# A planned kernel (mLSTM and a gated feed-forward layer): another picture of transposing transfers, the output's store on another engine, and the order found anew

## The chip, the cores and the metric

The kernel runs on one core of one Trainium2 chip. The metric is the device time of one execution in microseconds (us). A core has engines that run side by side, each through its own list of instructions in program order: PE (TensorE, the matmuls), DVE (VectorE), ACT (ScalarE), POOL (GpSimd) and SP (SyncE, which here only issues DMA transfers). They wait for each other by semaphores.

## The reference

Two parts follow each other. First an mLSTM for B = 4 batches, H = 8 heads, S = 768 steps and head size D = 40:

```python
for t in range(S):
    m_new = np.maximum(f_gate[:, :, t] + m, i_gate[:, :, t])
    f_stab = np.exp(f_gate[:, :, t] + m - m_new)
    i_stab = np.exp(i_gate[:, :, t] - m_new)
    C = f_stab * C + i_stab * np.einsum('bhd,bhe->bhde', vt, kt)
    n = f_stab * n + i_stab * kt
    h_tilde = np.einsum('bhde,bhe->bhd', C, qt)
    denom = np.maximum(np.abs(np.einsum('bhd,bhd->bh', n, qt)), 1.0)
    y[:, :, t] = sigmoid(o_gate) * h_tilde / denom
```

Then, for each of the 3072 tokens x (320 wide, all heads side by side):

```python
h = x @ w_in                                 # 320 -> 1024
e = np.exp(h - h_max)
solu = h * e / (e.sum() + 1e-9)
ln = (solu - mu) / np.sqrt(var + 1e-6) * g_ln
out = ln @ w_out                             # 1024 -> 320
```

## The kernel before

**Units.** The sequence is cut into 6 chunks of 128 steps. A unit u is one batch's chunk: 128 tokens, all 8 heads; there are 24, the batch running fastest, so unit u needs the state that unit u − 4 left. In each unit (line numbers of the kernel before):

- tk (L917) loads the tokens' values, keys and queries; el and er (L920, L930) load gate sums from DRAM. DVE reduces tk to the queries' size (am, L962), ACT and DVE cast the queries into a high and a low half (qs, L982 and L990), and a transposing DMA brings them into qT (L1006).
- d: PE makes the exponents of the gates in two groups of four heads (L1021) in psum buffers named sy, ACT takes the exponential (L1033), POOL masks it (L1047). PE makes the scores (L1092), DVE multiplies them with the masks (L1104), and PE makes the inter-chunk part from the state (y, L1129) and the intra-chunk part (L1155). DVE divides (x, L1193), and POOL multiplies with the output gate's sigmoid sg (L1205); the sigmoid is taken once for four units (L1064).
- The state: PE's update (L1220) goes into the psum buffer sx. DVE copies it in two halves into cs (L1248), and POOL and two DMA copies finish it. There is one buffer sx, and the transposes of x (L1284) use it too. ACT and DVE cast the transposed x into a high half xh (L1289, L1290) and a low half xl (L1295, L1303).
- The feed-forward layer: 16 matmuls into ph (L1338), DVE's row maximum nm (L1395), ACT's exponential e (L1402), DVE's sums and product (s, sb from L1411; e, L1456), ACT's squares sq (L1467), DVE's short z and ab (L1477 to L1480). POOL raises to the power −1/2 (pw, L1488). ACT casts the result to half precision (us, L1526), POOL makes the low part (L1502), and a transposing DMA brings both into big (L1505). 24 matmuls go into the psum buffer so_ (L1542; one buffer), ACT scales that into ot (L1564), and a DMA stores it (L1569).

The weights are loaded and split ahead of it, in blocks: w_in, and w_out (L747 loads, L632 casts on ACT, L788 is DVE's centring, eight operations).

**The order.** Nothing is emitted where it is written. Each piece is recorded with `P.op` on an engine, with a duration in ns, what it writes and reads, and a priority. `Plan.run` then simulates the engines: it takes the engine whose next piece can start first, and of the pieces on it that could start within 25 ns of each other the one of lowest priority. Each engine's program is the order so found, and the chip keeps to it. The priority is `rank`: the table RANK has three numbers for each kind of work, one for all units, one weighted to the first four and one weighted to the last four. When a buffer comes round again, the plan makes its next user wait for all users of the last.

DMA has a picture of its own in the plan: an issue on its engine for some ns, and for all transfers together one "dma" time, to which each transfer adds its `after`. A transposing transfer is marked swift. `load` records an ordinary one.

While the weights are prepared the plan also puts matmuls of no use on idle PE (L1583): 65 of them, before and after the change alike.

Of the kernel before, what the change touches and what calls it, by code (L numbers as in the profile page):

```python
# [49 lines left out]
RANK = {  # L50
    "dve hv": (-8.77, 9.26, 4.82),
    "act dl": (0.78, 2.31, -4.35),
    "sp cs": (0.07, -14.3, 2.82),
# [11 lines left out]
    "sp qT": (-13.44, -12.38, -6.71),
    "act d": (-5.4, -18.84, 4.87),
    "pool kt": (45.57, 11.55, -3.27),
    "pe ps": (6.61, 6.35, 2.41),
    "dve p": (-10.23, 3.52, -0.65),
    "pe sy": (-15.11, 18.49, 0.7),  # L70
    "dve y": (10.14, -9.76, 58.33),
    "dve rd": (11.26, -29.28, -6.47),
    "dve yi": (-27.2, 3.12, 7.54),
    "dve x": (-13.73, 20.42, 8.34),
    "pool x": (14.62, 16.05, -18.49),
    "pe sx": (17.0, -10.7, -3.08),
    "pool ct": (9.82, 3.17, -12.23),
    "dve cs": (3.16, 13.11, -5.46),
    "pool cs": (4.66, 7.11, -21.22),
    "pool c": (20.35, 9.11, -0.97),  # L80
    "act xh": (-12.03, -10.17, 10.98),
    "dve xl": (-2.53, 7.81, -4.99),
    "pe ph": (8.0, 18.89, 1.01),
    "dve us": (-8.44, -1.71, -1.62),
    "dve s": (21.3, 0.3, -5.21),
    "dve nm": (1.05, 9.93, -11.02),
    "act e": (12.47, -4.96, 3.73),
    "dve e": (9.73, -0.84, 5.75),
    "act sq": (13.33, -14.19, 1.37),
    "dve z": (-7.83, -3.7, -12.59),  # L90
    "dve ab": (6.33, 8.39, -12.11),
    "pool pw": (23.96, -7.55, 0.11),
    "dve so": (3.54, 5.69, 11.85),
    "act us": (-22.64, -5.39, -9.02),
    "pool us": (9.91, 12.1, -2.77),
    "sp big": (-4.83, -9.5, -2.73),
# [1 line left out]
    "act ot": (13.32, -27.18, 14.42),
    "sp ot": (-7.0, -11.66, 1.0),
    "sp w_in": (10.76,),  # L100
    "sp w_out": (-3.76,),
    "w_in": (-10.15,),
    "w_out": (-19.4,),
    "w_mul": (7.44,),
}
# [9 lines left out]
class Plan:  # L115
# [51 lines left out]
    def run(self):  # L167
# [174 lines left out]
def mlstm_moe_kernel(ctx: ExitStack, tc: tile.TileContext, tok, og, fg, ig, w_in, w_out, gln, out):  # L342
    nc = tc.nc
# [555 lines left out]
    def unit(u):  # L899
# [103 lines left out]
        op(
            SPQ,
            2500,
            lambda P: nc.sync.dma_start_transpose(  # L1006
# [204 lines left out]
        if c < NC - 1:  # L1211
# [313 lines left out]
        else:  # L1525
            op(ACT, 945, lambda P: nc.scalar.copy(out=P[us[0]][:, 0], in_=P[e]), [(*us[0], 0)], [e])  # L1526
# [42 lines left out]
        P.op(SPQ, 440, lambda P: nc.sync.dma_start(out=out[r : r + L, :], in_=P[ot]), [], [ot], rank(SPQ, "ot"), 440)  # L1569

# [58 lines left out]
```

## Time and profile before

| | |
|---|---|
| runs | 324.87, 323.91, 327.02 us; median 324.87 |
| profiled execution | 324.0 us, its span 322.3 us (1.7 us lie around it) |
| mean granted TensorE clock | 0.995 |
| busy: PE, DVE, ACT, POOL | 289.1, 270.3, 215.2, 172.0 us |
| DMA | 54.75 MB in 116498 packets, mean 170 GB/s |

In the rows of the trace SPq is SP's DMA queue, PEld PE's weight loads. A row begins with the start and length in us; a bracket at its end has the idle time of the engine ahead of it and what ended that. A line of the list of groups has the number of instructions, their busy time and the mean ns of one, and the idle time ahead.

### The profile page before, as it was taken

The page shows a single profiled execution, that of the slowest core. Times are in us where ns is not written, and L with a number is a line of the kernel's source. Part 1 is how long each engine was busy: PE and PEld are TensorE (multiplying, and loading weights), DVE is VectorE, ACT ScalarE, POOL GpSimd, SP SyncE. Part 2 cuts the span into 40 slices and gives each one's busy share as a digit, 9 for nine tenths or more (in the row PEclk, how much of TensorE's full clock was granted, in tenths as well). Part 3 has the DMA queues.
Part 4 walks back from the last instruction along what each step waited for, and adds up shares of the span by engine and source line. Part 5 has one row for each costly group of instructions (what it writes and reads, how often), then busy time and mean ns, then how long its engine had stood idle before and what let it go on. Part 6 is the DMA issues. An engine that isn't in the chain of part 4 may idle for free. (4 is left out here: it accounts for less than half of the span.)

```text
span 322.3 us, 6940 instructions
## 1 busy us (share of the span) xinstructions
PE 289.1 (90%) x2453; PEld 230.1 (71%) x2453; DVE 270.3 (84%) x702; ACT 215.2 (67%) x372; POOL 172.0 (53%) x193
## 2 busy tenths in 40 slices
PE   0499997989799997999989999999999999999965
PEld 0398774767588876688868778876888788777743
DVE  5995899999899888699987899986999979877540
ACT  4556966598975586775587757678655976665341
POOL 6002424457586844696673986474968534554300
PEclk9999999999999999999999999999999999999979
DMA  6789873564999987778979679796999776661631
GB/s 169 284 198 246 277 161 112 133 127 127 165 210 172 253 174 166 169 159 243 177 194 158 159 167 243 157 201 160 155 229 224 185 166 143 104 134 30 140 73 57
DMA packets 116498, 54.75 MB, mean 170 GB/s; under 512 B 103024, under 2 KB 110736, under 8 KB 116464
## 3 DMA queue, kind: packets, MB, share of 16 engines
q1 hardware_dynamic: 116464, 54.32, 75.9%
q8 instruction: 19, 0.31, 0.4%
q14 instruction: 15, 0.12, 0.2%
HBM read 21.66 MB, written 4.33 MB: 81 GB/s over the span
## 5 line engine op out<-in xcount | busy, mean ns | idle before, releaser
L1502 POOL TENSOR_TENSOR us<-e,us 128x1024 f16<-128x1024 f32 x23 | 49.3, 2142 | 57.8 <-ACT us L1526 52.1
L1542 PEld LDWEIGHTS <-big 128*128 128x128 f16 x576 | 60.0, 111 | 23.4 <-issue 4.3
L1155 PEld LDWEIGHTS sy<-tk,d 128*128 128x128 f32 x384 | 51.7, 192 | 3.8 <-DVE d L1104 1.4
L1155 PE MATMUL sy<-tk,d 128*128 128x41 f32 x384 | 52.0, 259 | 0.7 <-DVE d L1104 0.7
L982 ACT ACTIVATE qs<-tk,rr 128x640 f16<-128x640 f32 x48 | 37.6, 820 | 16.6 <-DVE rr L975 16.0
L1047 POOL TENSOR_SCALAR_AFFINE_SELECT d<-d 128x1024 f32<-128x1024 f32 x24 | 27.7, 1155 | 32.9 <-ACT dl L1043 32.0
L1205 POOL TENSOR_TENSOR x<-x,sg 128x320 f32<-128x320 f32 x24 | 23.0, 956 | 25.0 <-ACT d L1033 15.7
L1104 DVE SCALAR_TENSOR_TENSOR d<-sy,am,d 128x512 f32<-128x512 f32 x48 | 33.8, 745 | 1.8 <-POOL d L1047 1.3
L1033 ACT ACTIVATE d<-sy 128x512 f32<-128x512 f32 x48 | 28.2, 589 | 9.3 <-PE sy L1021 9.0
L1338 PE MATMUL ph<-wih,xh 128*128 128x512 f32 x96 | 32.1, 412 | 2.3 <-ACT xh L1290 2.1
L1526 ACT CAST us<-e 128x1024 f16<-128x1024 f32 x23 | 24.0, 1044 | 14.2 <-issue 4.3
L990 DVE SCALAR_TENSOR_TENSOR qs<-tk,rr,qs 128x320 f16<-128x320 f32 x48 | 29.2, 626 | 3.2 <-ACT qs L982 3.1
L1338 PE MATMUL ph<-wil,xh 128*128 128x512 f32 x96 | 30.3, 393 | 0.0
L1402 ACT ACTIVATE e<-ph,nm 128x1024 f32<-128x1024 f32 x23 | 25.5, 1109 | 6.8 <-DVE nm L1395 6.7
L1456 DVE SCALAR_TENSOR_TENSOR e<-ph,s,e 128x1024 f32<-128x1024 f32 x23 | 29.4, 1276 | 0.1
L1395 DVE TENSOR_REDUCE nm<-ph 128x1 f32<-128x1024 f32 x23 | 27.9, 1215 | 1.2 <-PE ph L1338 1.2
L1467 ACT ACTIVATE sq<-e,nmean 128x1024 bf16<-128x1024 f32 x24 | 27.5, 1144 | 0.6 <-DVE nmean L1446 0.6
L1338 PE MATMUL ph<-wih,xl 128*128 128x512 f32 x96 | 26.7, 398 | 0.0
L962 DVE TENSOR_REDUCE am<-tk 128x1 f32<-128x640 f32 x24 | 19.4, 810 | 3.3 <-DMA tk<-in_tok_dram 3.3
L1338 PEld LDWEIGHTS ph<-wih,xh 128*128 128x128 f32 x96 | 17.0, 189 | 6.6 <-ACT xh L1290 3.4
L1021 PE MATMUL sy<-er,el 128*128 128x512 f32 x48 | 20.8, 437 | 0.8 <-DMA er<-gd 0.5
L1338 PEld LDWEIGHTS ph<-wil,xh 128*128 128x128 f32 x96 | 18.0, 188 | 4.3
(199 smaller groups left out, 698.1 us busy)
## 6 DMA issues: line engine op xcount, KB each, us to landing
tk<-in_tok_dram SPq DMA_DIRECT2D x24, 484.0 KB
sg<-in_og_dram SPq DMA_DIRECT2D x12, 320.0 KB
out_dram<-ot SPq DMA_DIRECT2D x24, 160.0 KB
big<-in_w_out_dram SPq DMA_DIRECT2D x4, 640.0 KB
cs<-cs SPq DMA_DIRECT2D x20, 102.5 KB
big<-in_w_in_dram SPq DMA_DIRECT2D x4, 512.0 KB
cs<-c SPq DMA_DIRECT2D x20, 51.2 KB
big<-in_w_in_dram SPq DMA_DIRECT2D x2, 256.0 KB
```

Of the source, the lines that this page charges most:

```text
L982: nc.scalar.activation(out=dst, in_=q_src(P, a).unsqueeze(2).to_broadcast([L, H, 2, D]), func=AF.Copy, scale=P[rr],)
L990: V.scalar_tensor_tensor(out=q_parts(P, a, 2 - a, 1), in0=q_src(P, a), scalar=P[rr], in1=q_parts(P, a, 0, 1), op0=ALU.mult, op1=ALU.subtract,)
L1033: lambda P, j=j, pd=pd: nc.scalar.activation(out=P[d_t][:, 4 * j : 4 * j + 4, :], in_=P[pd].rearrange("p (h l) -> p h l", l=L), func=AF.Exp,),
L1047: lambda P: nc.gpsimd.affine_select(out=P[d_t], in_=P[d_t], pattern=[[0, H], [1, L]], base=0, channel_multiplier=-1, compare_op=ALU.is_ge, ...
L1104: lambda P, j=j, ps=ps: V.scalar_tensor_tensor(out=P[p_t][:, 4 * j : 4 * j + 4, :], in0=P[ps].rearrange("p (h l) -> p h l", l=L), scalar=P ...
L1155: nc.tensor.matmul(yv(P)[:, h, :], lhsT=P[p_t][:, h, :], rhs=v1(P)[:, h, :], start=True, stop=True)
L1338: nc.tensor.matmul(P[ph][:, j * HF : (j + 1) * HF], lhsT=a, rhs=w[:, j * HF : (j + 1) * HF], start=n == 0, stop=n == 7,)
L1395: lambda P: V.tensor_reduce(out=P[nm], in_=P[ph], axis=AX.X, op=ALU.max, negate=True),
L1456: lambda P: V.scalar_tensor_tensor(out=P[e], in0=P[ph], scalar=P[sc], in1=P[e], op0=ALU.mult, op1=ALU.mult, accum_out=P[nmean]),
L1467: lambda P: nc.scalar.activation(out=P[sq], in_=P[e], func=AF.Square, bias=P[nmean], scale=-float(DFF), accum_out=P[su]),
L1502: eng.tensor_tensor(out=P[us[1]][:, 1, sl], in0=P[e][:, sl], in1=P[us[0]][:, 0, sl], op=ALU.subtract)
L1542: nc.tensor.matmul(P[po][:, 0:DM], lhsT=uTv(P, a)[:, k, :], rhs=P[w][:, k, :], start=g == 0 and i == 0, stop=g == 3 and i == len(some) - 1,)
```

## The change

The change has three parts, all in what the plan is told. The matmuls, their sizes and all other operations are the same in number and kind; the store alone is on another engine.

1. The plan's costs of DMA: a transposing transfer occupies the issuing SP for 1950 ns instead of 2500 (2600 for big), adds 2600 ns to the "dma" time instead of 2300, and holds SP until at most 1000 ns of "dma" time are left (DMA_LAST). Some issues and copies get other costs.
2. The output's store is issued by ACT (`nc.scalar.dma_start`) instead of SP.
3. RANK has new numbers in every row, and the row "sp ot" gives way to "act st". Two of its 54 rows are shown.

```diff
 RANK = {
...
-    "dve am": (11.35, -12.35, 10.1),
+    "dve am": (9.58, 14.08, 13.41),
...
-    "pe so_": (141.04, -13.8, -12.79),
+    "pe so_": (13.4, -5.9, -1.95),
...
+    DMA_LAST = 1000
...
                 if self.swift[n]:
                     free["dma"] = max(max(s + self.DMA_IN, t) + after, end + self.DMA_IN + self.DMA_SWIFT)
+                    free[eng] = max(end, free["dma"] - self.DMA_LAST)
...
     def load(ns, fn, out, inp=(), prio=0.0, behind=(), issue=450, eng=SPQ):
-        P.op(eng, issue if eng == SPQ else 100, fn, out, inp, prio, ns, 1.0, behind)
+        P.op(eng, issue if eng == SPQ else 240, fn, out, inp, prio, ns, 1.0, behind)
...
-        load(1500, lambda P: nc.sync.dma_start(out=P[tk], ...), [tk], issue=650, ...)
+        load(1700, lambda P: nc.sync.dma_start(out=P[tk], ...), [tk], issue=500, ...)
...
         op(
             SPQ,
-            2500,
+            1950,
             lambda P: nc.sync.dma_start_transpose(
...
-            after=2300,
+            after=2600,
             swift=True,
         )
...
-            op(PE, 500, upd, [pu], [kt, tk])
+            op(PE, 350, upd, [pu], [kt, tk])
...
-            load(300, lambda P: nc.sync.dma_start(out=P[cn][D : 2 * D], in_=P[cn][0:D]), ...
+            load(430, lambda P: nc.sync.dma_start(out=P[cn][D : 2 * D], in_=P[cn][0:D]), ...
...
-            op(SPQ, 2600, lambda P: tr_u(P, 0, 0, 2 * DFF), [uT[0]], ..., after=2300, swift=True)
+            op(SPQ, 1950, lambda P: tr_u(P, 0, 0, 2 * DFF), [uT[0]], ..., after=2600, swift=True)
...
-        P.op(SPQ, 440, lambda P: nc.sync.dma_start(out=out[r : r + L, :], in_=P[ot]), [], [ot], rank(SPQ, "ot"), 440)
+        load(480, lambda P: nc.scalar.dma_start(out=out[r : r + L, :], in_=P[ot]), [], [ot], eng=ACT, prio=rank(ACT, "st"))
```

How it moves the instructions is shown at four places. Line numbers of the changed kernel are 3 higher from L300 on.

**DVE, unit 7.** cs is unit 7's new state, copied in two halves out of sx, am the reduction of unit 10's tokens, nm, sb, s and ab belong to earlier units' feed-forward layers, d to a later unit's masked scores. Before:

```order
L1395 TENSOR_REDUCE nm<-ph 128x1
L1248 TENSOR_TENSOR cs_1553<-ct,sx 40x4x41
L962 TENSOR_REDUCE am<-tk 128x1
L1248 TENSOR_TENSOR cs_1553<-ct,sx 40x4x41
L1104 SCALAR_TENSOR_TENSOR d<-sy,am,d 128x512 x2
```

After:

```order
L1398 TENSOR_REDUCE nm<-ph 128x1
L1251 TENSOR_TENSOR cs_1556<-ct,sx 40x4x41
L1414 TENSOR_SCALAR sb<-nm 128x1
L1483 TENSOR_SCALAR ab<-z,su 128x1
L1251 TENSOR_TENSOR cs_1556<-ct,sx 40x4x41
L1420 TENSOR_SCALAR sb<-nm,sb 128x1
L1107 SCALAR_TENSOR_TENSOR d<-sy,am,d 128x512 x2
L1426 RECIPROCAL s<-sb 128x1
L965 TENSOR_REDUCE am<-tk 128x1
```

The reduction has left the place between the halves and stands behind the masked scores; two one-column operations stand between the halves.

**PE, unit 8.** so_ is the output of an earlier unit, ph unit 8's feed-forward layer, sy<-cs unit 9's inter-chunk part, sy<-tk,d its intra-chunk part, sy<-er,el the first exponents of unit 10. Before, from the last output matmul on:

```order
L1542 MATMUL so__1726<-woh,big 128x320
L1338 MATMUL ph<-wih,xh 128x512 x2
L1338 MATMUL ph<-wil,xh 128x512 x2
L1338 MATMUL ph<-wih,xh 128x512 x2
L1338 MATMUL ph<-wil,xh 128x512 x2
L1129 LDWEIGHTS qT
L1129 MATMUL sy<-cs_1194,qT 128x41
```

After, where the sixteen matmuls of the inter-chunk part and twelve of the intra-chunk part stand ahead of these rows, between the output matmuls:

```order
L1545 MATMUL so__1717<-woh,big 128x320
L1158 MATMUL sy<-tk,d 128x41 x4
L1024 MATMUL sy<-er_97,el_110 128x512
L1341 MATMUL ph<-wih,xh 128x512 x2
L1341 MATMUL ph<-wil,xh 128x512 x2
L1341 MATMUL ph<-wih,xh 128x512 x2
L1341 MATMUL ph<-wil,xh 128x512 x2
```

ph has moved behind unit 9's two parts and unit 10's first exponents.

**ACT, around unit 7's store.** ot is the scaled output, qs a later unit's queries, d its exponentials, us and sq belong to the feed-forward layer. Before:

```order
L1526 CAST us<-e 128x1024
L1467 ACTIVATE sq,su<-e,nmean 128x1024
L1564 ACTIVATE ot<-so__1726,so 128x320
L982 ACTIVATE qs_77<-tk,rr 128x8x80
L1033 ACTIVATE d<-sy 128x512
L982 ACTIVATE qs_77<-tk,rr 128x8x2x40
L1033 ACTIVATE d<-sy 128x512
```

After:

```order
L1567 ACTIVATE ot<-so__1717,so 128x320
L985 ACTIVATE qs_77<-tk,rr 128x8x80
L1036 ACTIVATE d<-sy 128x512
L1529 CAST us<-e 128x1024
L1572 DMA out_dram<-ot 128x320
L985 ACTIVATE qs_77<-tk,rr 128x8x2x40
L1470 ACTIVATE sq,su<-e,nmean 128x1024
L1036 ACTIVATE d<-sy 128x512
```

The store stands three instructions behind the one that makes its data, and ahead of the second half of qs, the squares and the second exponential.

**DVE, the warm-up.** wg holds the weights being centred, e is the feed-forward product: unit 1's x stands ahead of the centring before, and unit 0's e 21 rows behind it. Before:

```order
L1193 TENSOR_TENSOR x<-sy,rd 128x320
L962 TENSOR_REDUCE am<-tk 128x1
L788 SCALAR_TENSOR_TENSOR wg<-wg,g,so__415 128x320 x8
L1104 SCALAR_TENSOR_TENSOR d<-sy,am,d 128x512 x2
```

After, where x is unit 2's and e unit 0's:

```order
L1255 COPY cs_630<-sx 40x4x41
L1196 TENSOR_TENSOR x<-sy,rd 128x320
L1459 SCALAR_TENSOR_TENSOR e,nmean<-ph,s,e 128x1024
L791 SCALAR_TENSOR_TENSOR wg<-wg,g,so__433 128x320 x8
L807 TENSOR_REDUCE wmx<-wm 128x1
```

Unit 2's x and unit 0's e now come ahead of the centring.

More of the change, by code (lines that the diff above doesn't have):

```diff
@@ L65 @@
[L65 to L96, printed above, removed]
-    "pe so_": (141.04, -13.8, -12.79),
[L98 to L104, printed above, removed]
+    "dve hv": (23.33, 2.61, -8.41),
+    "act dl": (-13.89, 1.42, 15.86),
+    "sp cs": (15.71, -11.0, 1.49),
+    "sp el": (11.68, 7.73, 7.44),
@@ new lines @@
+    "sp er": (-14.42, 10.81, -1.73),
+    "pe d": (-7.78, -13.43, 0.84),
+    "pool d": (-3.94, 7.63, -1.66),
+    "sp tk": (-1.91, 3.44, 1.44),
+    "sp sg": (10.11, -8.82, 1.07),
+    "act sg": (12.05, 13.77, 6.95),
+    "dve am": (9.58, 14.08, 13.41),
+    "dve rr": (-44.3, 6.12, -5.12),
+    "act qs": (4.5, 10.92, 1.85),
+    "dve qs": (5.02, -8.56, 4.35),
+    "sp qT": (-10.03, -9.06, -9.39),
+    "act d": (-5.33, 1.71, -3.54),
+    "pool kt": (2.84, 7.78, -9.82),
+    "pe ps": (1.88, 9.06, 7.84),
@@ new lines @@
+    "dve p": (-14.56, -5.61, 13.82),
+    "pe sy": (-16.95, 18.59, -2.67),
+    "dve y": (20.48, -15.63, 7.53),
+    "dve rd": (-9.54, -6.86, 8.01),
+    "dve yi": (4.0, -10.27, 27.79),
+    "dve x": (-12.07, -11.05, -10.34),
+    "pool x": (-11.54, -1.11, -11.0),
+    "pe sx": (1.75, -7.41, -9.99),
+    "pool ct": (-1.29, 6.93, -5.48),
+    "dve cs": (-10.37, 16.2, -0.21),
+    "pool cs": (13.28, -7.65, -8.37),
+    "pool c": (9.07, 5.8, 12.81),
+    "act xh": (6.31, -4.21, -10.37),
+    "dve xl": (2.01, 1.31, 12.34),
@@ new lines @@
+    "pe ph": (-1.6, 13.15, 11.88),
+    "dve us": (-4.93, 0.64, 0.84),
+    "dve s": (9.63, 19.53, -15.99),
+    "dve nm": (-4.22, 13.66, -14.95),
+    "act e": (4.37, 4.67, -4.78),
+    "dve e": (23.45, -18.54, 13.22),
+    "act sq": (12.59, 7.72, -4.31),
+    "dve z": (12.84, -14.02, -0.14),
+    "dve ab": (14.29, 4.79, -5.46),
+    "pool pw": (14.77, -10.21, 9.54),
+    "dve so": (-7.85, 12.93, 8.07),
+    "act us": (-10.4, 22.99, 9.12),
+    "pool us": (3.79, 3.14, 6.37),
+    "sp big": (-5.11, -1.19, 6.47),
@@ L105 @@
+    "pe so_": (13.4, -5.9, -1.95),
+    "act ot": (8.14, 7.42, -15.22),
+    "act st": (6.77, 11.98, 2.63),
+    "sp w_in": (8.91,),
+    "sp w_out": (7.71,),
+    "w_in": (-1.64,),
+    "w_out": (-9.29,),
+    "w_mul": (-5.17,),
 }
@@ L914, in op @@
             P.op(eng, ns, fn, o, i, rank(eng, o[0][0]), after, busy, behind, mix, port, swift)
-        load(1500, lambda P: nc.sync.dma_start(out=P[tk], in_=tok[b, c * L : (c + 1) * L, :]), [tk], issue=650, prio=rank(SPQ, "tk"), behind=[("d", u - 2)] if u > 1 else [])
+        load(1700, lambda P: nc.sync.dma_start(out=P[tk], in_=tok[b, c * L : (c + 1) * L, :]), [tk], issue=500, prio=rank(SPQ, "tk"), behind=[("d", u - 2)] if u > 1 else [])
         load(
@@ L1273, in unit @@
             )
-            load(300, lambda P: nc.sync.dma_start(out=P[cn][D : 2 * D], in_=P[cn][0:D]), [(*cn, 2)], [(*cn, 0), (*cn, 1)], issue=830, prio=rank(SPQ, "cs"))
+            load(430, lambda P: nc.sync.dma_start(out=P[cn][D : 2 * D], in_=P[cn][0:D]), [(*cn, 2)], [(*cn, 0), (*cn, 1)], issue=830, prio=rank(SPQ, "cs"))
             load(200, lambda P: nc.sync.dma_start(out=P[cn][2 * D :, 0], in_=P[c3]), [(*cn, 3)], [c3], issue=830, prio=rank(SPQ, "cs"))
@@ L1527, in unit @@
             op(POOL, 2105, lambda P: lo_u(P, nc.gpsimd, slice(0, DFF)), [(*us[1], 1)], [e, (*us[0], 0)])
-            op(SPQ, 2600, lambda P: tr_u(P, 0, 0, 2 * DFF), [uT[0]], [(*us[0], 0), (*us[0], 1)], after=2300, swift=True)
+            op(SPQ, 1950, lambda P: tr_u(P, 0, 0, 2 * DFF), [uT[0]], [(*us[0], 0), (*us[0], 1)], after=2600, swift=True)
         po, ot = (("so_", u), ("ot", u))
```

13 lines of the change are left out of this document (removed).

## The prediction

> **What bounds the kernel now.** I read the page first (busy shares and the digit rows), then busy time by stages of 10 us, then TensorE's own rows with the idle time in front of them, and last the waits of the DMA queue.
>
> ```profile
> PE 289.1 (90%) x2453; PEld 230.1 (71%) x2453; DVE 270.3 (84%) x702; ACT 215.2 (67%) x372; POOL 172.0 (53%) x193
> DVE  5995899999899888699987899986999979877540
> 50.00:60.00 10.00, 7.80 (x59) 5.88 (x60) 9.89 (x33) 4.76 (x12) 4.03 (x5) 1.00 0.11 33
> 150.00:160.00 10.00, 10.00 (x98) 8.15 (x97) 9.35 (x27) 6.05 (x13) 7.66 (x8) 1.00 1.05 205
> ```
>
> The stage rows give, after the stretch and its length, the busy time of PE, weight loads, DVE, ACT and POOL with their counts, then the granted clock, the DMA share and GB/s. In the steady stage (150 to 160) PE is busy the whole 10.00 us, and DVE 9.35: PE sets the pace, and only two things can move the end there, PE's instructions and the idle time in front of them. The change leaves PE's instructions as they are. In the warm-up (50 to 60) it is the other way round: PE 7.80, DVE 9.89. There the order of DVE's work sets the pace. PE's idle time is 33.2 us (the span of 322.3 less 289.1); most of it is the start and the end. What lies between are these rows (start, length, engine, line, operation, and in brackets the idle time in front and what ended it):
>
> ```profile
> 121.47 0.82 DVE L962 TENSOR_REDUCE am<-tk 128x1 f32<-128x640 f32 x1 [1.11 <-DMA tk<-in_tok_dram]
> 122.32 0.33 DVE L1248 TENSOR_TENSOR cs<-ct,sx 40x164 f32<-40x164 f32 x1
> 122.79 0.30 PE L1284 MATMUL sx<-ident,x 128*128 128x128 f32 x1 [1.76 <-DVE cs L1248]
> 168.11 0.30 PE L1284 MATMUL sx<-ident,x 128*128 128x128 f32 x1 [0.83 <-DVE cs L1248]
> 212.92 0.41 PE L1284 MATMUL sx<-ident,x 128*128 128x128 f32 x2 [0.29 <-POOL pw L1488]
> 135.47 0.50 PE L1338 MATMUL ph<-wih,xh 128*128 128x512 f32 x1 [0.56 <-ACT xh L1290]
> 180.79 0.50 PE L1338 MATMUL ph<-wih,xh 128*128 128x512 f32 x1 [0.56 <-ACT xh L1290]
> 225.60 0.50 PE L1338 MATMUL ph<-wih,xh 128*128 128x512 f32 x1 [0.56 <-ACT xh L1290]
> L1155 PE MATMUL sy<-tk,d 128*128 128x41 f32 x384 | 52.0, 259 | 0.7 <-DVE d L1104 0.7
> L1395 DVE TENSOR_REDUCE nm<-ph 128x1 f32<-128x1024 f32 x23 | 27.9, 1215 | 1.2 <-PE ph L1338 1.2
> ```
>
> **Steady stage: −4.5 us.** The six PE rows wait 1.76 + 0.83 + 0.29 + 3 × 0.56 = 4.56 us, and each is a wait that the order itself makes.
>
> The first three are units 7, 11 and 15. The one psum buffer sx is held by the state update until DVE has copied both halves of it (L1248); only then can PE transpose x into it (L1284). In DVE's order the reduction am of a unit three further on stands between the halves. It waited 1.11 us for its tokens and ran 0.82, and the second half began at 122.32, right behind it. In the new order two one-column operations (sb, ab) stand there, and am comes behind the masked products d. That am waits where nothing in front of PE's next work is behind it. What is late next at this place is DVE's chain nm (1.22 by its group line), half a copy (0.33), sb, ab, half a copy (0.33) behind the last ph matmuls, some 3.0 us with an estimate of 0.3 for each short one and the latencies, against 3.2 us of PE's own work up to the transposes (the update, eight scores matmuls and two thirds of an output group). That slack of 0.2 is thin, so part may come back at each of the three.
>
> The other three are units 8, 12 and 16: ph stands right behind the previous output group and waits 0.56 for ACT's xh. In the new order the sixteen intra-chunk matmuls (52.0 / 24 = 2.2 us a unit by their group line, shared with the output group that runs between them) and the first exponent matmul come in between; that is more than 0.56, and the wait goes. I take 4.5 for the six, and +0.5 for new small waits at such places (0.15 to 0.2 at three of them); the ends are 0 (all come back elsewhere) and −4.56.
>
> **Warm-up: −1.6 us.**
>
> ```profile
> 71.62 0.31 PE L1542 MATMUL so__792<-woh,big 128*128 128x320 f16 x1 [1.05 <-DMA big<-us]
> 83.36 0.48 DVE L1193 TENSOR_TENSOR x<-sy,rd 128x320 f32<-128x320 f32 x1
> 83.98 1.05 POOL L1205 TENSOR_TENSOR x<-x,sg 128x320 f32<-128x320 f32 x1 [2.19 <-PE sx L1220]
> 85.73 0.31 PE L1542 MATMUL so__983<-woh,big 128*128 128x320 f16 x1 [2.29 <-DMA big<-us]
> 88.94 0.48 PE L1338 MATMUL ph<-wih,xh 128*128 128x512 f32 x1
> 26.59 0.59 SPq L747 DMA_DIRECT2D big<-in_w_out_dram  x1
> 32.25 0.78 ACT L632 ACTIVATE uc<-big 128x640 f32<-128x640 f32 x1 [0.55 <-DMA big<-in_w_out_dram]
> L788 DVE SCALAR_TENSOR_TENSOR wg<-wg,g,so__415 128x320 f32<-128x320 f32 x8 | 3.7, 542 | 0.0
> L1456 DVE SCALAR_TENSOR_TENSOR e<-ph,s,e 128x1024 f32<-128x1024 f32 x23 | 29.4, 1276 | 0.1
> ```
>
> PE waits 1.05 and 2.29 for the transposed activations of units 0 and 1, 3.34 in all. Two moves meet them. DVE does e of unit 0 ahead of the eight centring operations on the weights (3.7 us by their group line) and an am, which is an estimate of 4.5 us earlier for units 0 and 1; and PE has the output groups of units 0 and 1 later, behind the transposes and scores of later units. Both waits should go. What is late next is unit 4's x on DVE: ahead of it DVE has about 1.5 us more than before (unit 2's e at 1.28 is added, half a state copy, some short ones; one short one is gone), and DVE has no idle time worth naming there. x then starts at 83.36 + 1.5 = 84.9; its product on POOL starts 0.62 later as before (85.5), lasts 1.05 (86.5), and the transposes with an output group beside them take about 0.8: ph of unit 4 at 87.3 instead of 88.94. That is −1.6. The ends: −3.3 (both waits gone and x not late) and +4, if the w_out blocks, which SP issues behind more of the units' transfers, an estimate of 6 to 9 us later, arrive late. One such block took from 26.59 to 32.25 from issue to use, 5.7 us. I take −1.6, the chain of the rows, because DVE and PE also want the blocks later.
>
> **Start: 0.**
>
> ```profile
> 17.00 3.25 SPq L1006 DMA_TRANSPOSE qT<-qs  x1
> 22.65 0.48 SPq L930 DMA_DIRECT2D er<-gd  x1
> 26.86 0.47 PE L1021 MATMUL sy<-er,el 128*128 128x512 f32 x1 [0.46 <-DMA er<-gd]
> ```
>
> The first exponent matmul waits for er, issued at 22.65 behind the first transposing issue of 3.25 us and others. In the new order two el issues stand ahead of that transposing one and the identity block of i behind er: er may come up to 1 us sooner, but the transposing issue about 1.7 us later. One helps the exponents, the other delays unit 0's scores; DVE is busy with the weights beside it. 0, with ends −1 and +1.
>
> **The store on ACT: 0.**
>
> ```profile
> SPq L1505 <- POOL pw L1488: 30.2, 9, 9.1
> SPq L1569 <- ACT ot L1564: 11.8, 6, 3.7
> 150.40 0.41 SPq L1569 DMA_DIRECT2D out_dram<-ot  x1
> 175.86 0.95 SPq L920 DMA_DIRECT2D el<-bd  x1
> 126.59 0.47 PE L1021 MATMUL sy<-er,el 128*128 128x512 f32 x1
> 130.86 0.62 PE L1092 MATMUL sy<-qT 120*128 120x128 f16 x8
> 131.41 0.51 PE L1220 MATMUL sx<-tk,kt 128*40 128x41 f32 x16
> 128.44 0.60 ACT L1033 ACTIVATE d<-sy 128x512 f32<-128x512 f32 x1
> 128.94 1.11 ACT L1402 ACTIVATE e<-ph,nm 128x1024 f32<-128x1024 f32 x1
> L982 ACT ACTIVATE qs<-tk,rr 128x640 f16<-128x640 f32 x48 | 37.6, 820 | 16.6 <-DVE rr L975 16.0
> L1467 ACT ACTIVATE sq<-e,nmean 128x1024 bf16<-128x1024 f32 x24 | 27.5, 1144 | 0.6 <-DVE nmean L1446 0.6
> L1526 ACT CAST us<-e 128x1024 f16<-128x1024 f32 x23 | 24.0, 1044 | 14.2 <-issue 4.3
> ```
>
> On SP, 24 issues of 0.41 go, with their waits for ot (11.8 us in the first group of waits). That is worth nothing by itself: SP waits 30.2 us for the activations before the big transposing transfer, so it had time. On ACT the store stands behind the cast us and ahead of the second half of qs, sq and the second exponential. ACT is idle 322.3 − 215.2 = 107 us, and 24 × 0.41 = 9.9 us fit into that as a sum; but the place counts. PE's second scores group needs the psum buffer that the second exponential frees. ACT's chain from PE's first exponent matmul: 0.43 (matmul), then the first exponential 0.50 (the rows 128.44 and 128.94 start 0.50 apart), the cast 0.95 and qs 0.72 (their means less the overlap of 0.1), sq 1.14 with its sum, the second exponential 0.60: 4.35 us. PE's path from that matmul to its second scores group: 130.86 − 126.59 = 4.27, half the eight scores matmuls 0.27, and the update of about 0.45, which now stands ahead: 5.0. So 0.65 us of issue are hidden, and 0.41, the row of the same transfer on SP, is below that. Beyond 0.65 each further microsecond costs PE as much in about 18 of 24 units (every fourth has the gate's sigmoid on ACT and another order there; I leave those out). The ends: 0.41 costs 0; 0.95, what a small issue takes on SP behind a transposing one, costs 0.3 × 18 = +5.4. Below nothing it cannot go by more than SP's 0.41 at the end of a unit, which no PE row waits for. I take 0, since the store's own row is nearest.
>
> **The end: 0.**
>
> ```profile
> 309.85 0.30 PE L1542 MATMUL so__4415<-woh,big 128*128 128x320 f16 x1 [2.44 <-ACT ot L1564]
> 310.00:320.00 10.00, 8.37 (x48) 5.11 (x46) 0.81 (x5) 2.30 (x4) 0.55 (x1) 0.83 0.35 85
> ```
>
> The order of PE and ACT behind the last ph is the same in both but for the store, so the wait of 2.44 stays, and the last store is issued by the engine that made its data. 0.
>
> Behind that wait the granted clock fell to 0.83 for the stage, while it stayed 1.00 around the wait of 2.29 at 85.73. The Trainium skill, "TensorE: Matmul & The Clock Gate", section "What's actually happening", says that an idle window of about 3.4 us halves the clock until PE has been busy as long. The trace has a shorter wait that lowered it and one that did not; by that rule PE matmuls behind a warm-up wait of 3.4 us or more would run at half speed for 3.4 us, 1.7 us more as an estimate from the page, and the end of +4 there would be +5.7.
>
> **The sum.** On the profiled execution (324.0 us: span 322.3 and 1.7 around it) −4.5 + 0.5 − 1.6 + 0 + 0 + 0 = −5.6, 318.4. The median of the runs is 324.87, 0.87 above it; on that scale **319.3**, given as 319.2.
>
> **The rivals.**
>
> 1. *The waits only move.* DVE binds the warm-up, so if its total time ahead of unit 4 sets the pace, the 1.6 does not come, and if half of the steady 4.5 returns as waits for DVE's copies or ACT's xh, 2 remain: 324.9 − 2 = 322.9, 322 to 325. For it: DVE at 9.35 of 10 in the steady stage leaves 0.65 per 10 us. Against: each of the six waits has one cause, and between 150 and 160 PE has none.
> 2. *Slower: the store holds up ACT.* If the issue on ACT stays until DMA descriptors of a transposing transfer ahead of it have gone through, as small issues on SP take 0.95 behind one and a transposing one itself 3.25, everything behind it on ACT (qs, sq, the second exponential) is late. At 0.99 us per store (0.65 + 6.1 / 18) the gain is eaten; 1% slower than before is reached at about 1.2. With 2.1, the middle of 0.95 and 3.25, in half of the 18 units: 319.2 + 9 × 1.45 = 332, 328.5 to 345. Against: SP usually waits for its data when the store comes up. The Trainium skill's "TensorE: Matmul & The Clock Gate", section "Architectural detail: the array is 16× 32×32, not 1× 128×128", calls ACT's queue strict first-in first-out, so nothing would pass the held store; no run here shows a DMA on ACT's queue.
> 3. *The change does not do what it says.* The new costs are a picture of a chip; if the gain in the order is only in the picture and semaphores or DMA landings make other waits, the time stays at 324.9, 322 to 327.
>
> **How the numbers follow.** Forecast case 0.62 (316 to 321.5), rival 1 0.17, rival 2 0.13, rival 3 0.08. The forecast case and rivals 1 and 3 together reach from 315.5 to 325.5 and hold about 0.85; the bounds of the start (±1) and of the warm-up's better end are in it, and rival 2 is left out. A measurement of this kernel can tell about 1% from no change: 321.6 and 328.1. Faster: 0.62 with nothing of the others; within: 0.17 + 0.08, 0.25; slower: 0.13.
>
> **What would show it.** Right: no PE row at L1287 (the new number of L1284) with an idle time ended by the state copy, none at L1341 ended by xh in units 8, 12 and 16; PE's first output rows of units 0 and 1 without a wait for big; the store's row on ACT near 0.41 and PE's scores rows without a wait for ACT. Wrong: a row of the store on ACT over 0.65 with PE scores waiting for d, or for rr and qs behind it; a wait of ACT for the weight blocks longer than now; a gap of PE over 3 us ahead of 90.

## The result and the profile after

The changed kernel took 313.57 us (312.98 to 314.65) against 324.87 us; the ratio is 0.965, interval 0.956 to 0.973. That is 11.3 us less, twice the 5.7 us of the forecast and below its range. The profiled execution took 313.57 us, its span 311.8 us, 10.5 us less than before.

From the page, in the order of the rows shown of before:

```profile
span 311.8 us, 6949 instructions
PE 285.0 (91%) x2453; PEld 232.2 (74%) x2453; DVE 281.6 (90%) x702; ACT 213.9 (69%) x372; POOL 173.5 (56%) x193
DVE  5997999999999999999999999999999999976660
```

PE's idle time (span less busy) fell from 33.2 to 26.8 us. DVE's busy time rose by 11 us in a kernel that is 10 us shorter; a busy share alone would have been read the wrong way round (the last section shows what the 11 us are). By stages, with the columns of before (PE, weight loads, DVE, ACT, POOL, granted clock, DMA share, GB/s):

```profile
60.00:70.00 10.00, 7.47 (x57) 6.04 (x55) 9.84 (x28) 4.14 (x9) 5.92 (x6) 0.88 0.41 100
70.00:80.00 10.00, 9.40 (x61) 7.21 (x61) 9.88 (x22) 9.64 (x15) 5.96 (x6) 0.77 0.48 118
150.00:160.00 10.00, 10.00 (x99) 8.18 (x98) 9.82 (x27) 6.33 (x13) 6.81 (x9) 1.00 0.89 187
300.00:310.00 10.00, 6.84 (x48) 4.57 (x47) 2.25 (x9) 3.26 (x7) 0.55 (x1) 1.00 0.36 86
```

The clock fell in the warm-up (0.88 and 0.77), where in this profile of before it had stayed, and it stayed at the end, where before it had fallen to 0.83. In the clock's records of all profiles here it is either whole or at half, and up to the last matmul a stretch at half lasts 3.4, 6.8 or 10.2 us. PE's timeline at the two kinds of places of the steady stage, unit 7's transposes and unit 8's ph:

```profile
121.09 0.30 PE L1545 MATMUL so__1548<-woh,big 128*128 128x320 f16 x1
121.22 0.30 PE L1545 MATMUL so__1548<-wol,big 128*128 128x320 f16 x1
121.36 0.49 PE L1287 MATMUL sx<-ident,x 128*128 128x128 f32 x3
135.78 0.48 PE L1024 MATMUL sy<-er,el 128*128 128x512 f32 x1
136.09 0.63 PE L1341 MATMUL ph<-wih,xh 128*128 128x512 f32 x2
```

No bracket stands behind them: the waits of 1.76 and 0.56 are gone. And the rows show more. Two output matmuls start 0.137 apart, though each is drawn 0.30 long, since the ends are modelled. A bracket counts from the end that is drawn, so each wait behind such a matmul is 0.16 longer than its bracket, and a wait under 0.16 has no bracket at all. This is a row pair of before:

```profile
134.47 0.43 PE L1542 MATMUL so__1726<-woh,big 128*128 128x320 f16 x2
135.47 0.50 PE L1338 MATMUL ph<-wih,xh 128*128 128x512 f32 x1 [0.56 <-ACT xh L1290]
```

The second of the two output matmuls started at 134.61, ph at 135.47: 0.86 later, where 0.14 is usual. PE lost 0.72, not 0.56. I counted so through the **steady stage** (first ph of unit 5 to the last ph of unit 23): each distance between starts less what that pair of lines usually takes, all above 0.1 us added up. What a pair usually takes is read from its shorter distances over all these kernels. For before this gives 29 waits and 10.0 us, where the brackets of the stage add up to 5.8; for the changed kernel 6 waits and 0.9 us. (With the median distance of each pair as the usual one it is 24 waits and 9.2 us, and 4 waits and 0.5 us; the difference of the two kernels stays within 0.5.) What is left over is 190.0 to 191.1 us in the kernels below that I counted so, but for one (b_ph, 192.4, where the clock fell in the stage). The span then comes apart like this:

| | before | after | difference |
|---|---|---|---|
| start to the first ph of unit 5 | 103.0 | 104.1 | +1.1 |
| steady stage | 201.1 | 191.1 | −10.1 |
| of it waits of PE, from starts | 10.0 | 0.9 | −9.2 |
| last ph of unit 23 to the end | 18.2 | 16.6 | −1.5 |

### The profile page after: what moved, and what is told of

Read it like the earlier page. It is cut to its first block, busy times and chain, and to the rows that moved or that the text cites. A ratio compares the mean times of both kernels' runs of the same rounds, so it can differ in the third digit from the quotient of the medians.

```text
span 311.8 us, 6949 instructions
## 1 busy us (share of the span) xinstructions
PE 285.0 (91%) x2453; PEld 232.2 (74%) x2453; DVE 281.6 (90%) x702; ACT 213.9 (69%) x372; POOL 173.5 (56%) x193
## 5 line engine op out<-in xcount | busy, mean ns | idle before, releaser
L1505 POOL TENSOR_TENSOR us<-e,us 128x1024 f16<-128x1024 f32 x23 | 50.4, 2190 | 72.5 <-ACT us L1529 65.9
L993 DVE SCALAR_TENSOR_TENSOR qs<-tk,rr,qs 128x320 f16<-128x320 f32 x48 | 43.1, 904 | 0.8 <-ACT qs L985 0.4
L1050 POOL TENSOR_SCALAR_AFFINE_SELECT d<-d 128x1024 f32<-128x1024 f32 x24 | 26.9, 1121 | 27.9 <-ACT dl L1046 27.6
L985 ACT ACTIVATE qs<-tk,rr 128x640 f16<-128x640 f32 x48 | 39.0, 824 | 2.3 <-DVE rr L978 1.7
L1036 ACT ACTIVATE d<-sy 128x512 f32<-128x512 f32 x48 | 28.0, 585 | 11.4 <-PE sy L1024 11.3
L1341 PE MATMUL ph<-wih,xl 128*128 128x512 f32 x96 | 27.5, 408 | 0.0
L1470 ACT ACTIVATE sq<-e,nmean 128x1024 bf16<-128x1024 f32 x24 | 27.4, 1140 | 0.0
L1208 POOL TENSOR_TENSOR x<-x,sg 128x320 f32<-128x320 f32 x24 | 24.8, 1034 | 0.4 <-DVE x L1196 0.2
L1262 POOL TENSOR_TENSOR cs<-cs 40x328 f32<-40x328 f32 x20 | 15.3, 764 | 15.7 <-DVE cs L1255 15.7
L1024 PE MATMUL sy<-er,el 128*128 128x512 f32 x48 | 21.8, 457 | 0.0
L1341 PEld LDWEIGHTS ph<-wih,xl 128*128 128x128 f32 x96 | 18.6, 194 | 4.3
```

What stands on the lines that cost most here:

```text
L985: nc.scalar.activation(out=dst, in_=q_src(P, a).unsqueeze(2).to_broadcast([L, H, 2, D]), func=AF.Copy, scale=P[rr],)
L993: V.scalar_tensor_tensor(out=q_parts(P, a, 2 - a, 1), in0=q_src(P, a), scalar=P[rr], in1=q_parts(P, a, 0, 1), op0=ALU.mult, op1=ALU.subtract,)
L1036: lambda P, j=j, pd=pd: nc.scalar.activation(out=P[d_t][:, 4 * j : 4 * j + 4, :], in_=P[pd].rearrange("p (h l) -> p h l", l=L), func=AF.Exp,),
L1050: lambda P: nc.gpsimd.affine_select(out=P[d_t], in_=P[d_t], pattern=[[0, H], [1, L]], base=0, channel_multiplier=-1, compare_op=ALU.is_ge, ...
L1341: nc.tensor.matmul(P[ph][:, j * HF : (j + 1) * HF], lhsT=a, rhs=w[:, j * HF : (j + 1) * HF], start=n == 0, stop=n == 7,)
L1470: lambda P: nc.scalar.activation(out=P[sq], in_=P[e], func=AF.Square, bias=P[nmean], scale=-float(DFF), accum_out=P[su]),
```

## The experiments

Names with b_ are the kernel before with the named moves or additions, names with a_ the changed kernel with one thing changed. Ratios are to the kernel before on the same chip; its medians there were 322.5 to 323.9 us. Stage and end are from one profile each.

| kernel | stage | waits in it | end | median | ratio (interval) |
|---|---|---|---|---|---|
| b_st_act | 199.1 | 8.1 | 16.6 | 323.27 | 1.002 (0.998 to 1.007) |
| a_st_sp | 191.1 | 1.0 | 16.7 | 314.92 | 0.975 (0.969 to 0.981) |
| a_st4 | 203.4 | 13.4 | 19.4 | 332.56 | 1.029 (1.021 to 1.038) |
| b_am | 197.7 | 6.9 | 18.2 | 321.35 | 0.996 (0.993 to 1.000) |
| a_am_early | 193.3 | 3.2 | 18.0 | 317.05 | 0.981 (0.975 to 0.988) |
| b_ph | 210.6 | 18.2 | 18.2 | 335.81 | 1.037 (1.027 to 1.047) |
| b_all | 198.3 | 7.3 | 18.0 | 322.28 | 0.998 (0.994 to 1.001) |
| b_all2 | 196.6 | 5.7 | 16.5 | 319.94 | 0.993 (0.988 to 0.998) |
| picture_only | 208.5 | | 18.3 | 353.95 | 1.101 (1.090 to 1.111) |
| rank_only | 221.7 | | 15.4 | 363.89 | 1.128 (1.119 to 1.138) |
| a_clock | 191.0 | | 18.3 | 313.55 | 0.972 (0.965 to 0.979) |
| b_tail | 199.4 | | 16.5 | 322.84 | 0.999 (0.995 to 1.002) |
| a_again | 191.3 | 0.8 | 18.3 | 314.75 | 0.972 (0.967 to 0.976) |
| a_tail | 191.1 | | 15.6 | 312.66 | 0.967 (0.962 to 0.971) |

The theory was that the order of DVE's and PE's work made the gain. The first rival was that the store's leaving SP made it.

**The store's engine, both ways.**

```diff
 a_st_sp:
-... nc.scalar.dma_start(out=out[r : r + L, :], in_=P[ot]) ...
+... nc.sync.dma_start(out=out[r : r + L, :], in_=P[ot]) ...
 b_st_act: the same line of before, the other way round
```

> The changed kernel with its store issued by SP again, everything else in the same order. Theory A (the order of DVE's and PE's work made the gain): 313.6 us, within 1 us of the changed kernel; the stage from unit 5's first ph matmul to unit 23's last stays at 191 us. Theory B (the store's leaving SP made it, since SP waits for ot ahead of transposing transfers): a third or more of the 11.3 us comes back, 317.5 us or above, with PE waiting for qT or big.

> The kernel before with nothing changed but the store, issued by ACT at the place where the plan emitted it. Theory A: 324.9 us, within 1.5 us of the kernel before, the stage from unit 5 to unit 23 at 201 us. Theory B: 321 us or below. If a DMA issue holds ACT for its 0.3 to 0.4 us, units in which the store stands ahead of qs or the second exponential lose up to 0.4 us each, up to +4 us.

Neither moved: the stage is 191.1 with the store on SP as on ACT, and in before's order 199.1 with it on ACT, 199.4 with it on SP (b_tail, below; the 201.1 of the first profile is taken up under b_am). The ratio of b_st_act is 1.002, with an interval that holds 1, and that of a_st_sp 0.975, well below it. The rival is out, and since the changed program differs from before in the order and in the store's engine alone, the order made the gain. That the store's engine saved nothing that these runs can tell agrees with the Trainium skill, "DMA: Bandwidth & Descriptors", section "Issuing engines are not separate DMA queues", by which another issuing engine saves no more than the issue.

**The store on ACT in four pieces.** The rows of ACT in the changed kernel show that the issue runs beside the cast; the next piece starts right behind the cast, not behind the issue:

```profile
147.66 1.05 ACT L1529 CAST us<-e 128x1024 f16<-128x1024 f32 x1
147.74 0.34 ACTq L1572 DMA_DIRECT2D out_dram<-ot  x1
148.62 0.83 ACT L985 ACTIVATE qs<-tk,rr 128x640 f16<-128x640 f32 x1
```

```diff
-nc.scalar.dma_start(out=out[r : r + L, :], in_=P[ot])
+[nc.scalar.dma_start(out=out[r + q : r + q + 32, :], in_=P[ot][q : q + 32]) for q in range(0, L, 32)]
```

> The changed kernel with each store issued in four pieces of 32 rows, all on ACT: 4 x 0.34 = 1.4 us of issue instead of 0.34. If an issue runs beside the instruction that ACT has under way (the cast of 1.05 us ahead of it), about 0.3 to 0.4 us is left to hold ACT, under the slack of 0.65, and the time stays at 313.6 within 1.5 us. If an issue holds ACT for its length, PE's second scores group is 0.7 us late in some 18 units: 326.

```profile
156.12 1.05 ACT L1529 CAST us<-e 128x1024 f16<-128x1024 f32 x1
156.20 1.74 ACTq L1572 DMA_DIRECT2D out_dram<-ot  x4
157.99 0.83 ACT L985 ACTIVATE qs<-tk,rr 128x640 f16<-128x640 f32 x1 [0.82 <-ACT us L1529]
```

In this unit the four take 1.74 (0.43 each, more than I put in), and what goes beyond the cast holds ACT for 0.82. In other units of the stage the same four take up to 3.18 and hold it for up to 2.26. PE's scores then wait for the second exponential: 0.23 to 0.40 us in five units of the stage, where the hold is 0.82 to 1.22, 0.85 to 1.74 in seven, where it is 1.23 to 2.26, and 3.41 once ahead of the stage. In eleven of the twelve units the wait is 0.4 to 0.6 us shorter than the hold by its bracket, and 0.16 less than that by the starts. So there is a slack, but it is below the forecast's 0.65; the change's single issue, hidden under the cast, does not use it. The time, 332.6, is above the figure for an issue that holds ACT throughout, because the issues were longer than forecast and because the stage holds only 12.3 of the 21.1 us by which the span grew; 6.0 lie ahead of it and 2.8 behind it.

**am moved in before, and moved back in the changed kernel.**

```diff
 b_am: DVE, units 7, 11, 15
 L1248 TENSOR_TENSOR cs<-ct,sx
-L962 TENSOR_REDUCE am<-tk
 L1248 TENSOR_TENSOR cs<-ct,sx
 L1104 SCALAR_TENSOR_TENSOR d<-sy,am,d x2
+L962 TENSOR_REDUCE am<-tk
 a_am_early: the same row of the changed kernel, moved back behind the first half
```

> The kernel before with three DVE instructions moved: the reduction am of units 10, 14 and 18 goes from between the two state copies to behind the masked scores, as in the changed kernel. By the idle times in PE's rows (1.76 + 0.83 + 0.29) the stage from unit 5 to unit 23 falls by 2.9 us. By the spacing of PE's starts, where a wait counts from the usual distance of two output matmuls (0.137) and not from the modelled end (0.30), the waits are 1.92 + 0.99 + 0.45 and it falls by 3.4. If the waits only move, by less than 1.5. Time 321.5 to 322.

> The changed kernel with one of its moves undone: the reductions am of units 10, 14 and 18 back between the two state copies. By the theory (DVE's second copy frees the psum buffer for x's transposes) each costs PE the 0.8 us of am less what slack there is, up to 0.2: the stage from unit 5 to unit 23 at 192.9 to 193.6 instead of 191.1; if am also waits for its tokens there, 194.5. If that place does not matter in the changed kernel, 191.1 to 191.5.

b_am's stage fell from 201.1 to 197.7, by 3.4, as the starts say and not as the brackets do. But this is against one profile of before. Two other profiles with the same order up to there (b_st_act, b_tail) have stages of 199.1 and 199.4, because am waited less for its tokens: PE's waits at these places were 0.93 and 1.02 at the first and 0.24 or nothing at the others. Against those am is worth 1.4 to 1.7, and the medians say 1.1, with an interval that reaches no change. In the changed kernel the move back cost 2.2, with this row three times:

```profile
121.64 0.52 PE L1287 MATMUL sx<-ident,x 128*128 128x128 f32 x3 [0.66 <-DVE sb L1420]
```

The bracket puts it down to sb, the last short one before; the state copy that frees the psum buffer ended right there. 0.66 + 0.16 is about the 0.80 of am: the slack is nearly nothing.

**ph moved in before, alone and with what it needs.** b_ph moves two ph groups of units 8, 12 and 16 on PE. b_all adds the move of b_am, and takes DVE's masked scores of the next unit ahead. b_all2 also takes the exponential e on ACT and the product e on DVE ahead, as the changed kernel has them.

```diff
 b_ph: PE, unit 8 (12, 16)
-L1338 ph<-wih,xh / wil,xh (8 matmuls), behind the output group
+the same 8, behind L1129 sy<-cs, L1155 sy<-tk,d and the next L1021
 b_all: b_am, b_ph, and DVE
+L1104 d<-sy,am,d x2 (unit 9), behind L1417 sb
 L1480 ab, L1423 s, L1477 z, L1456 e
-L1104 d<-sy,am,d x2 (unit 9)
 b_all2: b_all, and on ACT and DVE
+L1402 e (unit 6), behind L1064 sg       +L1477 z, L1456 e, ahead of L1295 xl
-L1402 e (unit 6), behind L1033 d        -L1477 z, L1456 e, behind L1193 x
```

> The kernel before with six pieces of PE moved: the first two ph groups of units 8, 12 and 16 go behind the next unit's inter- and intra-chunk matmuls and an exponent matmul, as in the changed kernel. By the idle times in the rows (3 x 0.56) the stage from unit 5 to unit 23 falls by 1.7 us. By the spacing of starts (0.83 at the first ph matmul and 0.11 at the next, three times) by 2.8. If the waits only move, by less than 0.8. Time 322 to 323.2.

> The kernel before with the DVE move of the run b_am, the PE move of the run b_ph, and a third move: DVE's masked scores of units 9, 13 and 17 go ahead of four to five short operations and a product e of 1.3 us, to where the changed kernel has them. The theory after the last runs (the ph move alone put PE in front of a psum buffer that DVE still had to free, 2.31 us three times; the moves belong together): no PE wait of over 0.5 us at units 8, 12 and 16, and the stage from unit 5 to unit 23 falls from 201.1 by 3.4 for am and by 1.5 to 2.8 for ph, to 195 to 196.5. Rival (what is late next on DVE, e two units earlier, holds PE up again): 198 or more, no better than the run b_am (197.7).

> The kernel before with the moves of the run b_all and two more, as in the changed kernel: in units 8, 12 and 16 ACT's exponential e (of the unit two before) goes right behind the output gate's sigmoid instead of five pieces later, and DVE's product e goes ahead of the cast xl, so that it no longer stands ahead of the masked scores of units 9, 13 and 17. If the 0.83 us that was left at the intra-chunk matmuls (waiting for POOL's mask, which waits for DVE) was this product's 1.3 us, the ph half now pays: no PE wait over 0.3 us at units 8, 12 and 16, the stage from unit 5 to unit 23 at 194 to 195.5. If the wait only moves once more, 197 to 198.5.

PE's rows at the place, unit 9, in b_ph, b_all and b_all2:

```profile
138.24 0.33 PE L1129 MATMUL sy<-cs,qT 120*128 120x41 bf16 x7 [2.31 <-DVE d L1104]
```

```profile
135.68 0.42 PE L1155 MATMUL sy<-tk,d 128*128 128x41 f32 x2 [0.83 <-POOL d L1047]
```

```profile
136.01 0.41 PE L1155 MATMUL sy<-tk,d 128*128 128x41 f32 x2 [0.44 <-POOL d L1047]
```

The move alone made the kernel 3.7% slower: PE no longer waited 0.56 for xh but 2.31, three times, for the psum buffer that DVE's masked scores free. At two of these waits the granted clock fell to half, for 6.8 us (from 185.4) and 10.2 us (from 233.1), where before had 1.00:

```profile
185.00:193.00 8.00, 8.00 (x34) 6.96 (x33) 4.36 (x15) 3.13 (x6) 4.76 (x5) 0.57 0.53 117
233.00:244.00 11.00, 10.83 (x53) 9.37 (x53) 5.50 (x18) 4.28 (x7) 5.91 (x7) 0.53 0.50 107
```

PE sets the pace there, so by estimate these 17.1 us at half speed cost up to 8.5 of the 9.5 us by which the stage grew, and the waits themselves only about 1; the 18.2 in the table contain distances stretched by the clock. The four runs of b_ph had mean clocks of 0.950 to 0.979, so none shows the move without that loss. (The 0.83 in that expectation should read 0.72, as above.) With DVE's move PE waited 0.83 at the next place, for POOL's mask; b_all was no better than b_am alone, as its rival said. With ACT's and DVE's e moved too it waited 0.44, and the stage of 196.6 lies between the two theories. So the wait for xh was no mishap of one place: what could stand ahead of ph waits for DVE and POOL, and with three engines reordered PE still waits 0.60 there (from the starts) where it had waited 0.72 for xh. The 1.1 us between the stages of b_am and b_all2 is less than the 2 us by which profiles of one order differ, so a gain from the ph half is not shown clear of that. Most of the remaining 5.5 us between b_all2 and the changed kernel are waits: from the starts, three of 0.60 at these places (1.8 together), six of 0.16 to 0.30 some 10 us behind them (1.4), and twelve of 0.1 to 0.5 behind 255 us (2.4), against 0.9 in the changed kernel. Which move took each of them away was not tried.

**The table and the picture apart.**

```diff
 picture_only: the changed kernel with the RANK of before and the store on SP
 rank_only:    before with the new RANK and the store on ACT
```

> The old RANK and the store on SP, with the new picture of DMA in the plan. In its order am stands behind both state copies in units 7, 11 and 15 (with other DVE work between the halves), and ph behind the next unit's parts. Theory 1 (the picture alone makes orders that fit): the stage from unit 5 to unit 23 at 191 to 195, the time 313 to 318. Theory 2 (table and picture fit only as a pair): new PE waits of over 1 us at several units, 200 or more, the time above 323.

> The new RANK and the store on ACT, with the old picture of DMA in the plan. Theory 1 (the picture is what matters): waits like those of the kernel before, 198 to 202 for the stage from unit 5 to unit 23, the time 321 to 326. Theory 2 (the table and the picture fit only as a pair): 203 or more, above 326. Theory 3 (the table alone does it): 191 to 193, 313 to 316.

Either half alone is much slower than before, by 10% and 13%. Much of that lies ahead of the steady stage: unit 5's first ph comes at 120.3 and 123.2 instead of 103.0, and the stage takes 7.4 and 20.6 us more. The waits of PE in rank_only are, among others, for a big transfer at the end, for masked scores and for xh:

```profile
PE so__4451 L1542 <- DMA big<-us: 5.5, 1, 5.5
PE sy L1129 <- DVE d L1104: 5.5, 7, 1.5
PE ph L1338 <- ACT xh L1290: 5.4, 7, 1.3
```

The gain is in the one order that table and picture find together. Nothing in it says that the new picture is the truer one.

**The clock in the warm-up.**

```diff
+            if u == 2 and ns == (0, 1): 8 matmuls xh x w_in into ph, each start=True, stop=True
             for n in ns:
```

> The changed kernel with eight matmuls of no use put in front of unit 2's first ph group (1.9 us), so that PE does not idle between 61 and 66 us, ahead of the stretch of half clock from 67.8 to 74.5. If that stretch costs time, unit 5's first ph comes up to 3.3 us earlier (100.8 instead of 104.1) and the whole is 310 to 312. If DVE, which has no gap from 30 to 85, sets the pace there, the clock goes up and unit 5's first ph stays within 0.7 us of 104.1, the whole within 1 us of the changed kernel.

```profile
60.00:70.00 10.00, 9.14 (x65) 7.40 (x62) 9.84 (x31) 4.46 (x10) 5.70 (x6) 1.00 0.43 93
70.00:80.00 10.00, 7.19 (x59) 4.78 (x58) 9.85 (x17) 9.94 (x15) 6.46 (x5) 1.00 0.43 107
```

The clock is back at 1.00 (0.88 and 0.77 without), DVE's 9.84 and 9.85 are much as without it (9.84 and 9.88), and unit 5's first ph came at 103.7 (103.5 to 104.3 in five profiles without it). Half speed on PE cost nothing that these runs can tell, and DVE, which has no gap there, set the pace.

**The end.**

```diff
 b_tail: ahead of unit 22's first output matmul
+t = P.tags["sx"][1]()
+for _ in range(10): nc.tensor.matmul(t[:, 0:L], lhsT=P[I], rhs=P[I], start=True, stop=True)
 a_again: no change
 a_tail: ACT
+L1567 ot (unit 21), behind unit 21's last output matmul
 L1515 us (unit 23) x2
-L1567 ot (unit 21)
         and
-po, ot = (("so_", u), ("ot", u))
+po, ot = (("sx", ("o", u)) if last else ("so_", u), ("ot", u))
```

> The kernel before with ten matmuls of no use (some 2.2 us, into the idle psum buffer sx) put in the last long wait, 2.44 us ahead of unit 22's output matmuls. If the half clock behind that wait costs the end its 1.5 us (the stretch from unit 23's last ph to the end is 18.2 us before, 16.6 after the change), the clock stays at 1.00 in the last 12 us and that stretch becomes 16.6 to 16.9. If the last transposing transfers set the end anyway, it stays at 18 within 0.4.

> The changed kernel itself, unchanged, on the same chip as the run below. The stretch from unit 23's last ph to the end took 16.6 to 16.7 us in six profiles of either order and 18.0 to 18.3 in seven others. If that is chance (where the wait of 2.66 us falls in the window that the clock watches), it is one of these two again, and the start (first ph of unit 5 at 103.5 to 104.1) and the stage to unit 23 (191.1) stay.

> The changed kernel with its end loosened: ACT scales unit 21's output ahead of the two casts of unit 23 instead of behind them, and unit 23's output goes into the psum buffer sx, which is idle by then, so that it need not wait for unit 22's. If the wait of 2.66 us is what makes the end long and sometimes lowers the clock, it goes: unit 22's output starts about 2 us earlier, the stretch from unit 23's last ph to the end is 14.5 to 16 us with a clock of 1.00 in it, and the whole is 0.5 to 2 us below the changed kernel. If the last transposing transfers set the end, the stretch stays at 16.3 or above.

(Of the profiles named there, five had 16.5 to 16.7 and seven 18.0 to 18.3; the two others are a_st4 and rank_only.) Each of the seven, and a_again, has 3.4 us at half clock in its end, and none of the five has. The wait does not decide it: it is 2.44 in b_st_act and 2.66 in a_st_sp, with a short end, and 2.44 in b_all and 2.66 in a_clock, with a long one. b_tail, without the wait, had 16.5, and so had b_all2 with it, so b_tail alone decides nothing; its time was that of before (0.999). a_again is the changed kernel and has the long end. Its row, and the two stages that differ, a_again first and a_tail second:

```profile
301.51 0.30 PE L1545 MATMUL so__4415<-woh,big 128*128 128x320 f16 x1 [2.66 <-ACT ot L1567]
300.00:310.00 10.00, 7.87 (x45) 5.11 (x46) 2.63 (x10) 3.11 (x6) 0.55 (x1) 0.83 0.36 85
```

```profile
299.97 0.31 PE L1545 MATMUL so__4415<-woh,big 128*128 128x320 f16 x1 [1.33 <-DMA big<-us]
300.00:310.00 10.00, 7.02 (x48) 4.42 (x48) 2.43 (x10) 3.02 (x6) 0.55 (x1) 1.00 0.43 102
```

The same wait of 2.66 us stood in the first profile of the change without any loss of clock. In six runs of a_again the span was 311.6 or 311.7 twice (mean clock 0.995) and 313.0 to 314.0 four times (0.982 to 0.984). So 1.5 us of the difference between the two profiles is chance, in either order. a_tail takes the long wait away; unit 22's output now waits 1.33 for its transposing transfer instead, and the end is 15.6, below both. Its median is 2.1 us under a_again's on the same chip; the intervals of the two ratios still overlap.

## Why the prediction was right or wrong

- **What bounds it**: right. PE in the steady stage, DVE in the warm-up (a_clock).
- **Steady stage, −4.5 and +0.5 for new waits**: this step failed, in its size: −4.0 was forecast, −10.1 measured. The six waits went. For the three at the state copies a_am_early bears out the reason given, but shows a slack of nearly nothing instead of 0.2. But the sum was of six brackets, 4.56. From the starts the same six places held 5.9 with the matmuls right behind them, and twenty others, all but one with a bracket under 0.15 or none, another 4.2. The 0.5 of new waits did not come at these places. Measured: −9.2 in waits, −10.1 in all. The size also hangs on the execution: against the two other profiles of before's stage it is −8.0 and −8.3.
- **"Each is a wait that the order itself makes"**: true, but not one by one. b_ph, b_all and b_all2 show that the ph waits come back elsewhere when only PE is reordered, and shrink when DVE and ACT are reordered too; they are gone only in the whole new order. I had read the new order on PE alone for that term; rival 1 is what happens if only that part is done.
- **Warm-up, −1.6**: not borne out. PE's waits for big of units 0 and 1 did go, but in their place came waits for kt (1.08), xh (0.77), masks (0.69 and 0.55), ot (0.56) and qT (0.54). Unit 4's x was 2.4 us later instead of 1.5, and its first ph came at 90.8 instead of the forecast's 87.3. The pair of profiles says +1.1 up to unit 5. Seven profiles of before's order have unit 5's first ph at 103.0 to 106.2 (median 104.5), six of the changed order at 103.5 to 104.3 (median 103.9): the medians differ by 0.6 the other way, the ranges overlap, and a pair cannot tell.
- **Start, 0**: not borne out at its own rows. The first exponents came at 25.33 instead of 26.86 and unit 0's first scores at 26.55 instead of 28.07, 1.5 us sooner and beyond the end of −1; the delay from the transposing issue did not show. The same holds in every profile of the two orders (24.5 to 25.5 against 26.6 to 27.4). Unit 5's first ph shows almost none of it, which fits DVE setting the pace in between (medians 103.9 and 104.5).
- **The store, 0**: right in size (a_st_sp, b_st_act). The slack of 0.65 was put too high (a_st4: 0.4 to 0.6 by brackets, less by the starts); that the issue would not even use it, since it runs beside the cast, I had not seen. Rival 2's slowdown appeared only with issues some five times as long (a_st4).
- **The end, 0**: the wait stayed as forecast (2.66); the 1.5 us is the clock's chance, not a gain. The Trainium skill, "TensorE: Matmul & The Clock Gate", section "What's actually happening", wants an idle window of about 3.4 us for a fall of the clock; here 2.4 to 2.7 us were enough in some executions and not in others of the same kernel. In the prediction I had the two waits of before (2.44 with a fall, 2.29 without) and took it for a property of the place.
- **Rival 3** (the order's gain is only in the picture): no for the pair. For the halves, yes: an order found for one picture with another's table lost 10% and more.

## What to carry to other kernels

Where matmuls are pipelined and drawn longer than their spacing, measure PE's lost time from the distances between starts, by kind of pair, and over a whole stage; brackets gave 5.8 of 10.0 us here. A wait in a kernel ordered by a planner belongs to the order of several engines: moving the waiting piece alone brought a longer wait, and half clock behind it, and cost 3.7% where 0.7 us at three places had been at stake. Look at the granted clock of a slower run before you put its time down to a wait. And before crediting a change with the last microsecond, look at two profiles of the same order; start and end alone moved by 3 and 1.7 us.

## What the runs showed that I had not expected

- A DMA issue of 0.34 us on ACT's queue ran beside ACT's instruction under way and cost ACT nothing; four in a row (1.74) held it for the 0.82 that went beyond, and for up to 2.26 where they took longer.
- Half clock on PE for 6.8 us in the warm-up cost nothing that could be measured, because DVE set the pace; behind a wait of 2.66 us at the end 3.4 us of it cost 1.7 us in some executions and did not occur in others; behind waits of 2.31 us in the steady stage of b_ph it cost more than the waits.
- DVE's lower half of qs took longer with the new order while DVE's other large groups were alike: 0.63 us on the mean before, 0.90 after (the first two rows, before first), 13.9 us in all. The traces show what it meets. 18 of the 48 take more than 0.6 us in the changed kernel and 8 before; each of these began while a wide instruction of POOL was running and ended 0.34 to 0.35 us behind that one's end (the last two rows are such a pair, POOL's end at 140.16, DVE's at 140.51). All others took 0.53 to 0.56. So DVE's added busy time is waiting for POOL, which the profile counts as busy. No run moved POOL's work to test it.

```profile
L990 DVE SCALAR_TENSOR_TENSOR qs<-tk,rr,qs 128x320 f16<-128x320 f32 x48 | 29.2, 626 | 3.2 <-ACT qs L982 3.1
```

```profile
L993 DVE SCALAR_TENSOR_TENSOR qs<-tk,rr,qs 128x320 f16<-128x320 f32 x48 | 43.1, 904 | 0.8 <-ACT qs L985 0.4
```

```profile
138.01 2.15 POOL L1505 TENSOR_TENSOR us<-e,us 128x1024 f16<-128x1024 f32 x1 [3.03 <-ACT us L1529]
138.76 1.75 DVE L993 SCALAR_TENSOR_TENSOR qs<-tk,rr,qs 128x320 f16<-128x320 f32 x1
```
